# Packs of the first tokens and weights moved whole, gate columns with the biases, and a new order, in a gated mix of a spectral filter and an MLP

## The chip, the cores and the metric

The kernel runs on one core of one Trainium2 chip. The metric is the device time of one execution in microseconds (us). Before the change it is 372.66 us, the median of three runs (372.43 to 373.08).

## The reference

```python
def _A_ref(x, w_r, w_i):
    B, S, D = x.shape
    X = rfft2(x, axes=(-2, -1))
    W = w_r + 1j * w_i
    X = X * W
    return irfft2(X, (S, D), axes=(-2, -1))

def _B_ref(x, w1, b1, w2, b2):
    h = einsum("bsd,df->bsf", x, w1) + b1
    h = gelu(h)                                   # tanh form
    return einsum("bsf,fd->bsd", h, w2) + b2

x = A_x                                           # 1 x 2048 x 512
g = sigmoid((x * gate_w).sum(-1, keepdims=True))
return g * A_ref(x, A_w_r, A_w_i) + (1 - g) * B_ref(x, B_w1, B_b1, B_w2, B_b2)
```

x has 2048 tokens of 512 features, the MLP has 1792 hidden features. All arrays are float32.

## The kernel before

**Precision.** Each float32 operand of a matmul is split into a high part (names ending in h) and a low part (ending in l), both in the 12-bit format fp32r, and a product is made of three: high by high, high by low, low by high. A rounding to the high part is a copy with a cast, on ScalarE (ACT) or VectorE (DVE); the low part is a subtraction on DVE. TensorE (PE) does all products.

**The work.** The MLP is done for four columns of tokens c of 512 tokens, each made of four blocks of 128 tokens (j = c, c+4, c+8, c+12), and in two halves of seven blocks of 128 hidden features (f). For each f there is an up-product of 12 matmuls of 512 columns (tile ph, weights wa), a gelu with the bias b1t (line 1182, in place in ph), a split into g_h and g_l, and down-products (tile po, weights wb). The spectral part makes for each block j a transform along the features (tile pd, tables cf; two more columns of cf hold the gate's weights, so that the gate's logits come out of the same product), one along the tokens (py), radix-4 stages and the filter on DVE, and the way back (pz, pa). Both are mixed with the gate and written to out.

**How the order is made.** `tile_kernel` lists steps with an engine, a cost, a delay, the buffers that they read and write, and a rank (`Graph.add`). `Graph.schedule` (line 224) then plays the steps through with these costs; each engine takes the ready step of lowest rank. The ranks are the table RANKS (line 347), one number for each step, which replaces the ranks given at the steps (lines 1314 to 1316). The result is a fixed order of instructions for each engine; a number of the table tells a reader nothing by itself. SP (SyncE) issues nearly all transfers, in its own order; a transfer waits there until one of eight places for transfers under way is free and until its target buffer has been read.

**The start.** TensorE first multiplies zeros (`warm`, line 609; ZEROS = 8 products of 512 columns into the tile none). The first up-products need four packs of 256 KB:
- xa and xb hold the blocks 0 and 4 of the tokens; xa has the first two quarters q of the features, xb the last two. xa comes as two transfers of 128 KB, the first issued by ACT (line 624), the second by SP (line 625). xb (line 626) carries in each row four columns of the gate's weights besides its 512 numbers.
- war0 and war1 hold the weights of f = 0 and f = 1; war0 has the quarters 0 and 1, war1 the quarters 2 and 3 (`load_pack`, line 1101). war0 comes as two transfers of 128 KB, one for each f (line 1112), war1 as one (line 1108).

`split_packs` (line 676) rounds the packs: xa one half on ACT, one on DVE (lines 685, 686), xb on ACT (line 687). `load_pack` rounds war0 in two halves on ACT (line 1117), war1 one half on DVE and one on ACT (lines 1115, 1117). In `mlp` (line 1149) the up-products of f = 0 and 1 in column 0 are cut into passes of 12 matmuls of 256 columns: the first needs xa and war0, the second xb and war1, and two more need the tokens xr8 and xr12 (blocks 8 and 12). In the rows of the order and the profile, mxh and mxl are the split tokens, wa0h, wa0l, wa1h, wa1l the split packs of weights.

From xb's gate columns DVE works out the gate's columns of cf (gs, gq, lines 638 to 652). b1t, the biases, is loaded in `load_small` (line 655).

Of the kernel before, what the change touches and what calls it, by code (L numbers as in the profile page):

```python
# [17 lines left out]
P = 128  # L18
# [100 lines left out]
ZEROS = 8  # L119
# [56 lines left out]
class Graph:  # L176
# [281 lines left out]
)  # L458


# [907 lines left out]
```

## Time and profile before

| | |
|---|---|
| median of three runs | 372.66 us (372.43 to 373.08) |
| the profiled execution | 372.77 us, its span 370.8 us |
| instructions | 5551 |
| PE, PEld, DVE, ACT, POOL busy | 363.5, 307.4, 325.8, 235.2, 44.1 us |
| granted TensorE clock, mean | 0.998 |
| read from and written to HBM | 38.64 MB, 23.73 MB |

The span is the time from the first to the last instruction of the profiled execution; 2.0 us of its 372.77 lie around it. PE is TensorE's matmuls, PEld its weight loads, which run beside them. L12 is line 12 of the kernel; most matmuls stand under L536, a helper, so they are told apart by tile. Rows of the timeline give start, length (both us), engine, line, operation, output<-input, shape and count, and in brackets the idle time before with what ended it. In the chain of waits each row is start, length and what. Matmuls overlap, so the length of a row is longer than the distance to the next. A row of busy time by stretch gives the stretch, its length, the busy time of PE, PEld, DVE, ACT and POOL (with counts), the granted clock, the share of the DMA engines' time and GB/s.

### The profile page before, as it was taken

What the parts mean: (1) busy time and instruction counts of PE and PEld (TensorE: products, weight loads), DVE (VectorE), ACT (ScalarE), POOL (GpSimd) and SP (SyncE); (2) the same over time, 40 slices, a digit from 0 to 9 for tenths busy, and PEclk for the clock granted to TensorE, in tenths of its full rate; (3) what the DMA queues carried; (4) which work ended last, traced back from release to release, by engine and by line L of the source; (5) the groups of instructions that cost most, each with busy time, mean ns of one, the idle gap of its engine ahead of it and who ended that gap; (6) DMA issues with size and microseconds to landing.
All of it is one profiled execution on the core that took longest, in us unless ns stands there. A gap on an engine that the chain in (4) does not pass through costs nothing.

```text
span 370.8 us, 5551 instructions
## 1 busy us (share of the span) xinstructions
PE 363.5 (98%) x1799; PEld 307.4 (83%) x1799; DVE 325.8 (88%) x691; ACT 235.2 (63%) x464; POOL 44.1 (12%) x54
## 2 busy tenths in 40 slices
PE   7999999999999999999999999999999999999994
PEld 5888888888888888888888888888888888888894
DVE  4999889999999779999999999788738885999995
ACT  5875788887669755354456322796497639748830
POOL 0000000000000001111022011000432123111041
PEclk9999999999999999999999999999999999999999
DMA  7972879434934323878399684207997899825378
GB/s 236 397 244 64 253 245 361 140 100 150 311 107 138 101 60 102 216 148 194 115 204 246 175 195 67 49 14 292 180 167 130 176 300 209 138 72 115 98 99 186
DMA packets 39916, 62.99 MB, mean 170 GB/s; under 512 B 4688, under 2 KB 17552, under 8 KB 39120
## 3 DMA queue, kind: packets, MB, share of 16 engines
q1 hardware_dynamic: 32544, 49.67, 41.1%
q0 software_dynamic: 7200, 12.85, 23.7%
q8 instruction: 14, 0.23, 0.2%
q10 hardware_dynamic: 144, 0.13, 0.1%
q14 instruction: 14, 0.11, 0.1%
HBM read 38.64 MB, written 23.73 MB: 168 GB/s over the span
## 4 chain that ended last, share of the span: by engine, by line
PE 95%; DVE 1%; DMA 1%; SPq 0%; ACT 0%; issue 0%
PE ph L536 41%; PE po L536 40%; PE pz L536 4%; PE pd L536 4%; PE pa L536 3%; PE py L536 3%; DMA xb<-in_x0g 1%; DVE uv L1039 0%; DVE y L1061 0%; SPq L1112 0%; DVE o L1249 0%; DVE o L1244 0%; DVE y L1058 0%; ACT mxh L687 0%; ACT od L1036 0%
## 5 line engine op out<-in xcount | busy, mean ns | idle before, releaser
L1182 ACT ACTIVATE ph<-ph,b1t 128x512 f32<-128x512 f32 x56 | 36.9, 658 | 57.1 <-PE ph L536 54.8
L993 DVE SCALAR_TENSOR_TENSOR pq<-y,al,sw 128x256 f32<-128x256 f32 x32 | 14.0, 481 | 11.3 <-ACT sw L989 7.3
L986 ACT ACTIVATE sw<-y,al 64x512 f32<-64x512 f32 x32 | 22.5, 719 | 0.8 <-DVE y L849 0.3
L945 DVE TENSOR_TENSOR m<-y,wf 128x514 f32<-128x514 f32 x32 | 20.4, 689 | 0.0
L527 POOL DMA_DIRECT2D wa7l<-in_w x1 | 1.0, 1015 | 146.2 <-PE po L536 146.2
L527 POOL DMA_DIRECT2D bacc<-o x12 | 10.6, 931 | 65.8 <-ACT o L1231 64.6
L1228 ACT ACTIVATE o<-po,b2t 128x512 f32<-128x512 f32 x16 | 10.8, 688 | 8.3 <-PE po L536 8.3
L1231 ACT ACTIVATE o<-po 128x512 f32<-128x512 f32 x12 | 7.1, 597 | 13.6 <-PE po L536 13.3
L799 ACT ACTIVATE y<-py 64x256 f32<-64x256 f32 x32 | 12.2, 380 | 4.1 <-PE py L536 3.6
L536 PEld LDWEIGHTS pd<-cf,eoh 128*128 128x128 f32 x64 | 11.2, 188 | 2.4 <-issue 0.5
L536 PE MATMUL pd<-cf,eoh 128*128 128x260 f32 x64 | 13.1, 289 | 0.0
L796 ACT ACTIVATE y<-py 64x256 f32<-64x256 f32 x32 | 12.1, 378 | 0.5
L1039 DVE TENSOR_TENSOR uv<-pa,od 128x512 f32<-128x512 f32 x16 | 10.8, 685 | 0.5 <-ACT od L1036 0.3
L1036 ACT ACTIVATE od<-pa 128x512 f32<-128x512 f32 x8 | 4.8, 598 | 9.5 <-PE pa L536 9.3
L726 DVE TENSOR_TENSOR eo<-xr 128x256 f32<-128x256 f32 x28 | 10.8, 417 | 0.0
L536 PE MATMUL pd<-cf,eol 128*128 128x130 f32 x64 | 10.6, 251 | 0.0
L536 PEld LDWEIGHTS pd<-cf,eol 128*128 128x128 f32 x64 | 10.1, 188 | 0.2
L989 ACT ACTIVATE sw<-y 1x512 f32<-1x512 f32 x16 | 9.8, 627 | 0.4
L745 DVE TENSOR_TENSOR eol<-xr,eoh 128x512 fp32r<-128x512 f32 x12 | 8.2, 688 | 2.1 <-ACT eoh L744 2.0
L742 DVE TENSOR_TENSOR xr<-eo 128x256 f32<-128x256 f32 x24 | 9.7, 419 | 0.2
L527 POOL DMA_DIRECT2D out<-ba x8 | 7.0, 873 | 19.1 <-DVE ba L1083 7.6
L674 DVE TENSOR_TENSOR mxl<-xm,mxh 128x512 fp32r<-128x512 f32 x12 | 8.1, 686 | 1.3 <-ACT mxh L673 1.2
(717 smaller groups left out, 1339.0 us busy)
## 6 DMA issues: line engine op xcount, KB each, us to landing
wf<-in_wf SPq DMA_DIRECT2D x16, 257.0 KB, 3.6
bacc<-o SPq DMA_DIRECT2D x16, 256.0 KB, 3.1
xr<-in_xt SPq DMA_DIRECT2D x14, 256.0 KB, 3.4
wbr<-in_w SPq DMA_DIRECT2D x14, 256.0 KB, 3.7
war<-in_w SPq DMA_DIRECT2D x13, 256.0 KB, 4.5
xm<-in_xt SPq DMA_DIRECT2D x12, 256.0 KB, 5.3
bacc<-o POOLq DMA_DIRECT2D x12, 256.0 KB, 5.5
ba<-bacc SPq DMA_DIRECT2D x12, 256.0 KB, 2.7
```

What stands on the lines that cost most here:

```text
L527: return add("pool", kb / 150, 3.4, lambda: nc.gpsimd.dma_start(dst(), src(), accum_op=ALU.add), reads, writes, rank)
L536: pe.matmul(ps, w, x, start=start, stop=stop)
L726: v(lambda s=s, op=op: vec.tensor_tensor(eo.ap()[:, s], x.ap()[:, 0:2] if x else pack(0)[:, j // 4], x.ap()[:, 2:4] if x else pack(1)[:, j ...
L796: a(lambda o=o, i=i: act.activation(apart(0, o, HP), py.ap()[i:i + HP, 1].rearrange("p (a b) -> p a b", a=2), AF.Copy), HD, [py], [(Y[j], ...
L799: a(lambda o=o, i=i: act.activation(Y[j].ap()[o:o + HP, 1, :HD], py.ap()[i:i + HP, 0], AF.Copy, scale=-1.0), HD, [py], [(Y[j], 1 + k)], 0, ...
L945: v(lambda mk=mk, k=k, y=y, w=w: vec.tensor_tensor(mk.ap(), y.ap()[:, :, :ND], w.ap()[:, k:k + 1, :ND].to_broadcast([P, 2, ND]), op=ALU.mu ...
L986: a(lambda sw=sw, y=y, o=o, i=i: act.activation(sw.ap()[o:o + HP], y.ap()[i:i + HP, ::-1, :HD], AF.Copy, scale=al.ap()[i:i + HP, 0:1]), 51 ...
L989: a(lambda sw=sw, y=y, j=j: act.activation(sw.ap()[HP:HP + 1], y.ap()[HP:HP + 1, ::-1, :HD], AF.Copy, scale=math.cos(math.pi * j / NJ)), 5 ...
L993: v(lambda sw=sw, pq_=pq_, y=y, j=j, k=k, op=op: vec.scalar_tensor_tensor(pq_.ap()[:, k], y.ap()[:, k, :HD], al.ap()[:, 1 + j:2 + j], sw.a ...
L1039: v(lambda i=i, op=op: vec.tensor_tensor(uv.ap()[:, :, i], ps.ap()[:, 0], od.ap(), op=op), 512, [ps, od], [(uv, i)], 2)
L1182: a(lambda f=f, ps=ps: act.activation(ps.ap(), ps.ap(), AF.Gelu_apprx_tanh, bias=b1t.ap()[:, f:f + 1]), 600, [b1t], [ps], 0.9 if half else ...
L1228: a(lambda o=o, ps=ps, q=q: act.activation(o.ap(), ps.ap(), AF.Identity, scale=-1.0, bias=b2t.ap()[:, q:q + 1]), 600, [b2t, ps], [o])
```

## The change

xa, xb, war0 and war1 each come as one transfer of 256 KB, with the arrays laid out on the host so that each is contiguous. xa is issued whole by ACT, the other three by SP. The four gate columns move from xb into b1t, whose load is put ahead of the tables cf; gs is worked out from b1t. xa is rounded whole by DVE; war1 is rounded in two halves by ACT; the low part of war0 is one subtraction in place of two. One more product of zeros is made. RANKS is another table, so the order of all engines is another.

```diff
--- before.py
+++ after.py
@@ -116,7 +116,7 @@
 SPARE = 0.4
 LATE_SUMS = 1.5
 SOON, SPARE_SOON = 9.0, 0.05
-ZEROS = 8
+ZEROS = 9
 LATE_X = 1
 FOLD_DMA = 16
 RING, TI, TTAB = 3, 3, 3
@@ -345,116 +345,116 @@
 
 
 RANKS = (
-    -12312, -8112, -8674, 633, -8711, -11188, -8567, -11292, -9604, 821, 28, 1653, 2308, 731, 3074, 20, 536, -776,
...
+    -7460, -11155, -8172, -325, -8181, -8896, -8776, -8458, -190, 742, -779, 427, -287, 2439, 1452, 1057, 2055, 171,
...
 )
@@ -526,8 +526,8 @@
         reads = [*reads, buf("ring", [1], cls=len(g.steps))]
         return add("pool", kb / 150, 3.4, lambda: nc.gpsimd.dma_start(dst(), src(), accum_op=ALU.add), reads, writes, rank)
 
-    def dma_act(emit, kb, reads, writes):
-        return add("act", 0.4, kb / 390 + 2.2, emit, reads, writes, 0)
+    def dma_act(emit, reads, writes, lag):
+        return add("act", 0.4, lag, emit, reads, writes, 0)
 
     def raw(dst, src, q=sp):
         return q.dma_start(dst.bitcast(F32), src)
@@ -555,7 +555,7 @@
     def cf_of(c):
         return [(cft, c), (cft, 2), (cft, 3)]
 
-    b1t = one("b1t", [P, NF], pool=sa)
+    b1t = one("b1t", [P, NF + NQ], pool=sa)
     rev = one("rev", [P, NJ, 2, 2])
     b2t = one("b2t", [P, NQ])
     al = one("al", [P, 1 + NJ])
@@ -612,21 +612,21 @@
 
     add("pe", 0.427 * ZEROS + 0.05, 0.1, warm, [zero], [none], 0)
 
-    xa, xb = buf("z", [P, 2, 2, P], F32, "xa", parts=2), buf("xr", [P, D + NQ], F32, "xb")
+    xa, xb = buf("z", [P, 2, 2, P], F32, "xa", parts=2), buf("xr", [P, D], F32, "xb")
 
     def pack(k):
-        return xb.ap()[:, :D].rearrange("p (t q n) -> p t q n", t=2, q=2) if k else xa.ap()
+        return xb.ap().rearrange("p (t q n) -> p t q n", t=2, q=2) if k else xa.ap()
 
     def xblock(o, n):
         return x0g[o:o + P * n].rearrange("(p n) -> p n", n=n)
 
     add("vec", 0.2, 0.1, clear, [], Y, 0.7)
-    dma_act(lambda: act.dma_start(xa.ap()[:, 0].rearrange("p q n -> p (q n)"), xblock(0, HD)), 129, [], [(xa, 0)])
-    dma(lambda: sp.dma_start(xa.ap()[:, 1].rearrange("p q n -> p (q n)"), xblock(P * HD, HD)), 128, [], [(xa, 1)], 0, 2.5)
-    dma(lambda: sp.dma_start(xb.ap(), xblock(P * D, D + NQ)), 256, [], [xb], 0.02, 3.0)
+    dma_act(lambda: act.dma_start(xa.ap().rearrange("p t q n -> p (t q n)"), xblock(0, D)), [], [xa], 3.5)
+    dma(lambda: sp.dma_start(xb.ap(), xblock(P * D, D)), 256, [], [xb], 0.06, 3.3)
     XF = {}
     for j in NORD[2:4]:
         XF[j] = load_x(j)
+    dma(lambda: sp.dma_start(b1t.ap(), b1), 7, [], [b1t], 0.45)
     for c in range(2):
         dma(lambda c=c: raw(cft.ap()[:, c], cf_d[c]), 272, [], [(cft, c), (cft, 2), (cft, 3)], 0.6)
 
@@ -635,7 +635,7 @@
 
 
     for k, op in enumerate((ALU.add, ALU.subtract)):
-        tiny(lambda k=k, op=op: vec.tensor_tensor(gs.ap()[:, k], xb.ap()[:, D:D + 2], xb.ap()[:, D + 2:], op=op), [xb],
+        tiny(lambda k=k, op=op: vec.tensor_tensor(gs.ap()[:, k], b1t.ap()[:, NF:NF + 2], b1t.ap()[:, NF + 2:], op=op), [b1t],
              [(gs, k)])
     for k, op in enumerate((ALU.add, ALU.subtract)):
         tiny(lambda k=k, op=op: vec.tensor_tensor(gq.ap()[:, 0::3] if k else gq.ap()[:, 1:3], gs.ap()[:, :, 0], gs.ap()[:, :, 1], op=op),
@@ -652,7 +652,6 @@
     tiny(lambda: vec.tensor_tensor(gcol(1), four(), gcol(0), op=ALU.subtract), [gq, (cft, 2)], [(cft, 3)])
 
     def load_small():
-        dma(lambda: sp.dma_start(b1t.ap(), b1), 7, [], [b1t], 0.45)
         dma(lambda: sp.dma_start(b2t.ap(), b2), 2, [Y[0]], [b2t])
         add("vec", 0.1, 0.1, lambda: vec.tensor_scalar(b2t.ap(), b2t.ap(), -1.0, None, op0=ALU.mult), [], [b2t], 3)
         dma(lambda: sp.dma_start(rev.ap(), wrev), 32, [Y[0]], [rev])
@@ -682,8 +681,7 @@
         def both(b, k):
             return [(b, k), (b, 2 + k)]
 
-        a(lambda: act.activation(part(h, 0, 0), xa.ap()[:, 0], AF.Copy), 256, [(xa, 0)], [(h, 0)], 0)
-        v(lambda: vec.tensor_copy(part(h, 0, 1), xa.ap()[:, 1]), 256, [(xa, 1)], [(h, 2)], 0)
+        v(lambda: vec.tensor_copy(part(h, 0), pack(0)), 340, [xa], both(h, 0), 0)
         a(lambda: act.activation(part(h, 1), pack(1), AF.Copy), 512, [xb], both(h, 1), 0)
         for k, b in enumerate((xa, xb)):
             v(lambda k=k: vec.tensor_tensor(part(l, k), pack(k), part(h, k), op=ALU.subtract), 512, [b, *both(h, k)], both(l, k), 0)
@@ -1104,22 +1102,11 @@
             t = buf("wra", [P, D], F32, f"war{k}", parts=2)
             h, l = (buf("wa", [P, D], F32R, f"wa{k}{i}", parts=2) for i in "hl")
             PACK.append((h, l))
-            if k:
-                dma(lambda t=t: sp.dma_start(t.ap(), w1[1]), 256, [], [t], 0.05, 3.2)
+            dma(lambda k=k, t=t: sp.dma_start(t.ap(), w1[k]), 256, [], [t], 0.05 + k / 10, 3.2 if k else 3.0)
             for f in range(2):
                 u = slice(f * HD, (f + 1) * HD)
-                if not k:
-                    dma(lambda f=f, u=u, t=t: sp.dma_start(t.ap()[:, u], w1[0].rearrange("p d -> (p d)").rearrange("(f p d) -> f p d", f=2, d=HD)[f]),
-                        128, [], [(t, f)], 0.05, 2.8 + 0.2 * f)
-                if k and not f:
-                    v(lambda u=u, t=t, h=h: vec.tensor_copy(h.ap()[:, u], t.ap()[:, u]), HD, [(t, f)], [(h, f)], EARLY - 0.1)
-                else:
-                    a(lambda u=u, t=t, h=h: act.activation(h.ap()[:, u], t.ap()[:, u], AF.Copy), HD, [(t, f)], [(h, f)], EARLY - 0.1)
-                if not k:
-                    v(lambda u=u, t=t, h=h, l=l: vec.tensor_tensor(l.ap()[:, u], t.ap()[:, u], h.ap()[:, u], op=ALU.subtract), HD,
-                      [(t, f), (h, f)], [(l, f)], EARLY - 0.1)
-            if k:
-                v(lambda t=t, h=h, l=l: vec.tensor_tensor(l.ap(), t.ap(), h.ap(), op=ALU.subtract), D, [t, h], [l], EARLY - 0.1)
+                a(lambda u=u, t=t, h=h: act.activation(h.ap()[:, u], t.ap()[:, u], AF.Copy), HD, [(t, f)], [(h, f)], EARLY - 0.1)
+            v(lambda t=t, h=h, l=l: vec.tensor_tensor(l.ap(), t.ap(), h.ap(), op=ALU.subtract), D, [t, h], [l], EARLY - 0.1)
         for f in range(2):
             W["a", f] = None
 
@@ -1336,11 +1323,10 @@
     w1 = np.asarray(B_w1)[fold].reshape(NQ, P, NF, P).transpose(2, 1, 0, 3).reshape(NF, P, D)
     w2 = np.asarray(B_w2)[:, DORD].reshape(NF, P, D)
     b2 = np.asarray(B_b2)[DORD].reshape(NQ, P).T
-    b1 = np.asarray(B_b1).reshape(NF, P).T
     gw = np.asarray(gate_w)[fold].reshape(NQ, P).T
-    x0g = [xt[j, :, 2 * k:2 * k + 2].reshape(P, HD) for k in range(2) for j in (0, NJ // 4)]
-    x0g = np.concatenate([x0g[0].ravel(), x0g[1].ravel(), np.concatenate([*x0g[2:], gw], 1).ravel()])
-    w1 = np.concatenate([w1[:2, :, :HD].reshape(1, P, D), w1[:2, :, HD:].transpose(1, 0, 2).reshape(1, P, D), w1[2:]])
+    b1 = np.concatenate([np.asarray(B_b1).reshape(NF, P).T, gw], 1)
+    x0g = np.stack([xt[:NJ // 2:NJ // 4, :, 2 * k:2 * k + 2].transpose(1, 0, 2, 3) for k in range(2)]).ravel()
+    w1 = np.concatenate([np.stack([w1[:2, :, k * HD:(k + 1) * HD].transpose(1, 0, 2).reshape(P, D) for k in range(2)]), w1[2:]])
     wf = np.stack([np.asarray(A_w_r), np.asarray(A_w_i)], 1)
     back = (-np.arange(S)) % S
     rows = (P * np.arange(NJ)[:, None] + KROW) % S
```

SP's transfers at the start, before (war_93 and war_96 are war0 and war1, xr_100 and xr_105 the tokens xr8 and xr12, war_109 and wbr_113 the weights of f = 2 and of the first down-product):

```order
L625 DMA xa<-in_x0g 128x256
L1112 DMA war_93<-in_w 128x256 x2
L1108 DMA war_96<-in_w 128x512
L626 DMA xb<-in_x0g 128x516
L594 DMA xr_100<-in_xt 128x512
L594 DMA xr_105<-in_xt 128x512
L1140 DMA war_109<-in_w 128x512
L1140 DMA wbr_113<-in_w 128x512
L655 DMA b1t<-in_b 128x14
L1140 DMA wbr_131<-in_w 128x512
```

SP's transfers at the start now (war_78 and war_97 are war0 and war1, xr_99 and xr_101 xr8 and xr12):

```order
L1105 DMA war_78<-in_w 128x512
L625 DMA xb<-in_x0g 128x512
L1105 DMA war_97<-in_w 128x512
L594 DMA xr_99<-in_xt 128x512
L594 DMA xr_101<-in_xt 128x512
L1127 DMA war_103<-in_w 128x512
L1127 DMA wbr_105<-in_w 128x512
L629 DMA b1t<-in_b 128x18
L1127 DMA wbr_114<-in_w 128x512
L533 DMA cf<-cf 128x544
```

Five issues before xr8 became three, and xb went from the last of them to the second; war1 is now the last.

ACT at the same place, before (mxh_102 is the high part of the tokens):

```order
L624 DMA xa<-in_x0g 128x256
L606 ACT_TABLE_LOAD
L606 ACTIVATE gate<-zero 128x1
L685 ACTIVATE mxh_102<-xa 128x256
L1117 ACTIVATE wa0h<-war_93 128x256 x2
L1117 ACTIVATE wa1h<-war_96 128x256
L687 ACTIVATE mxh_102<-xb 128x2x256
L673 ACTIVATE mxh_102<-xr_100 128x512
```

ACT now:

```order
L624 DMA xa<-in_x0g 128x512
L606 ACT_TABLE_LOAD
L606 ACTIVATE gate<-zero 128x1
L1108 ACTIVATE wa0h<-war_78 128x256 x2
L685 ACTIVATE mxh_111<-xb 128x2x256
L1108 ACTIVATE wa1h<-war_97 128x256 x2
L672 ACTIVATE mxh_111<-xr_99 128x512
```

The rounding of xa left ACT, that of xb stands ahead of war1's, and both halves of war1 are ACT's.

TensorE's first passes, before (ph_0 and ph_1 are the up-products of f = 0 and f = 1):

```order
L536 MATMUL none<-zero 128x512 x8
L536 MATMUL ph_0_117<-mxh_102,wa0h 128x256 x2
L536 MATMUL ph_0_117<-mxl_107,wa0h 128x256 x2
L536 MATMUL ph_0_117<-mxh_102,wa0l 128x256 x2
L536 MATMUL ph_1_128<-mxh_102,wa0h 128x256 x2
L536 MATMUL ph_1_128<-mxl_107,wa0h 128x256 x2
L536 MATMUL ph_1_128<-mxh_102,wa0l 128x256 x2
L536 MATMUL ph_1_128<-mxh_102,wa1h 128x256 x2
L536 MATMUL ph_0_117<-mxh_102,wa1h 128x256 x2
L536 MATMUL ph_0_117<-mxl_107,wa1h 128x256 x2
L536 MATMUL ph_0_117<-mxh_102,wa1l 128x256 x2
```

TensorE's first passes now:

```order
L536 MATMUL none<-zero 128x512 x9
L536 MATMUL ph_0_118<-mxh_111,wa0h 128x256 x2
L536 MATMUL ph_1_124<-mxh_111,wa0h 128x256 x2
L536 MATMUL ph_0_118<-mxl_116,wa0h 128x256 x2
L536 MATMUL ph_1_124<-mxl_116,wa0h 128x256 x2
L536 MATMUL ph_0_118<-mxh_111,wa0l 128x256 x2
L536 MATMUL ph_1_124<-mxh_111,wa0l 128x256 x2
L536 MATMUL ph_1_124<-mxh_111,wa1h 128x256 x2
L536 MATMUL ph_1_124<-mxl_116,wa1h 128x256 x2
L536 MATMUL ph_0_118<-mxh_111,wa1h 128x256 x2
L536 MATMUL ph_0_118<-mxl_116,wa1h 128x256 x2
L536 MATMUL ph_1_124<-mxh_111,wa1l 128x256 x2
```

In the first pass f = 0 and f = 1 now alternate, where all of f = 0 stood first. In the second pass ph_1 with mxh and wa1h still opens; mxl follows after two products where it followed after four, and all eight products with wa1h now stand ahead of those with wa1l.

218 rows, old and new, of the table RANKS are left out of this document.

## The prediction

> **What bounds the kernel now.** I read the page's shares and its strip of slices first, then the list of what TensorE waited for, then the chain that ended last, then the first ten microseconds by engine.
>
> ```profile
> span 370.8 us, 5551 instructions
> PE 363.5 (98%) x1799; PEld 307.4 (83%) x1799; DVE 325.8 (88%) x691; ACT 235.2 (63%) x464; POOL 44.1 (12%) x54
> PE   7999999999999999999999999999999999999994
> PE 95%; DVE 1%; DMA 1%; SPq 0%; ACT 0%; issue 0%
> ```
>
> TensorE (PE) is busy in every slice but the first and the last. What it waited for, in the whole run, is three things, all at the start:
>
> ```profile
> PE ph L536 <- ACT mxh L687: 1.1, 1, 1.1
> PE none L536 <- DVE zero L604: 1.1, 1, 1.1
> PE ph L536 <- ACT wa0h L1117: 0.4, 1, 0.4
> ```
>
> The chain over the first 9 us (start, length, what) and over the end:
>
> ```profile
> 2.60 4.69 DMA xb<-in_x0g
> 7.31 0.64 ACT mxh L687
> 8.00 0.74 PE ph L536 x4
> ...
> 361.11 0.61 ACT od L1036
> 361.74 1.30 DVE uv L1039 x2
> ...
> 366.68 0.42 DVE o L1249
> ```
>
> So the time has three parts: the transfer of xb and its rounding on ScalarE up to 8.00; 353 us of matmuls without a wait; and a tail of some 10 us after 361.11. Both orders hold the same matmuls, but for one more warm-up product. A change at the start therefore moves the end by as much as it moves the point from which TensorE runs without a pause, if the new order keeps it fed.
>
> **Where that point is now.** TensorE's own rows (start, length, operation, idle before):
>
> ```profile
> 1.06 3.59 PE L536 MATMUL none<-zero 128*128 128x512 f32 x8 [1.06 <-DVE zero L604]
> 4.49 0.40 PE L536 MATMUL ph<-mxh,wa0h 128*128 128x256 f32 x2
> 8.00 0.74 PE L536 MATMUL ph<-mxh,wa1h 128*128 128x256 f32 x4 [1.14 <-ACT mxh L687]
> 9.32 0.40 PE L536 MATMUL ph<-mxl,wa1h 128*128 128x256 f32 x2
> 9.56 0.40 PE L536 MATMUL ph<-mxh,wa1l 128*128 128x256 f32 x2
> 9.80 0.40 PE L536 MATMUL ph<-mxh,wa0h 128*128 128x256 f32 x2
> ```
>
> A pair of 256-column products takes 0.24 (9.32 to 9.56 to 9.80), so 0.12 each. The products come in passes: first 12 that need the packs xa and war0, then 12 that need xb and war1 too, and at 9.80 the third pass, with the tokens xr8 and xr12. Twelve unhindered products take 1.44, so the second pass ran as if it had begun at 9.80 - 1.44 = 8.36.
>
> **What arrives when.** Busy time per stretch; the last column is GB/s of all transfers:
>
> ```profile
> 1.80:3.30 1.50, 1.50 (x5) 1.17 (x4) 0.01 (x1) 0.86 (x2) 0.00 (x0) 1.00 0.82 276
> 3.30:5.40 2.10, 2.10 (x10) 1.63 (x8) 1.31 (x3) 0.72 (x2) 0.00 (x0) 1.00 0.84 156
> 5.40:7.30 1.90, 1.06 (x7) 0.76 (x6) 0.72 (x2) 0.83 (x2) 0.00 (x0) 1.00 0.99 363
> 50.00:100.00 50.00, 50.00 (x252) 42.33 (x251) 48.12 (x115) 40.55 (x105) 0.00 (x0) 1.00 0.65 213
> ```
>
> The rate reaches 276, falls to 156 for 2.1 us, and is 363 afterwards. By 7.3, when xb is there, 1.5 x 276 + 2.1 x 156 + 1.9 x 363 = 1430 kB have come, of which xa, war0, war1 and xb are 1050; the other 380 belong to transfers issued behind them. Had the hole run at 363, the same bytes would have been there 1.2 us sooner.
>
> **The change, part by part.**
>
> The issues on SP (SyncE's queue):
>
> ```profile
> 0.74 0.39 SPq L625 DMA_DIRECT2D xa<-in_x0g  x1
> 1.19 0.89 SPq L1112 DMA_DIRECT2D war<-in_w  x2
> 2.12 0.43 SPq L1108 DMA_DIRECT2D war<-in_w  x1
> 2.60 0.46 SPq L626 DMA_DIRECT2D xb<-in_x0g  x1
> ```
>
> An issue takes about 0.45 whether it moves 128 KB or 256. Now two of five are gone: war0 goes out at 0.74, xb at 1.19, war1 at 1.65, all done at 2.08 instead of 3.06. The bytes of the four packs stay the same (the gate columns, 2 KB, leave xb). What was last is xb; now it is war1, issued 0.95 earlier than xb was (2.60 to 1.65).
>
> When war1 lands is the one large unknown. Lower bound: no hole and nothing from behind mixed in, 414 kB by 3.30 and the other 640 at 363, so 5.05. Upper bound: as late as xb now, 7.29, the sum of bytes being the same. Issues lay 0.45 apart while only 128 KB went with each, so part of the hole may be a lack of issued work, and part transfers that stood. I take the hole half filled, at (156 + 363)/2 = 260: it moves 546, so 960 kB are there by 5.40. Needed are the 1050 and between half and all of the 380 that mix in, 1240 to 1430 kB; at 363 that is 6.2 to 6.7, of which I take 6.5.
>
> What follows the landing on ScalarE and VectorE:
>
> ```profile
> 5.42 0.42 ACT L1117 ACTIVATE wa0h<-war 128x256 fp32r<-128x256 f32 x1 [1.24 <-DMA war<-in_w]
> 7.94 1.33 ACT L673 ACTIVATE mxh<-xr 128x512 fp32r<-128x512 f32 x2
> 3.29 0.29 DVE L686 CAST mxh<-xa 128x256 fp32r<-128x256 f32 x1 [2.19 <-DMA xa<-in_x0g]
> 3.90 0.70 DVE L689 TENSOR_TENSOR mxl<-xa,mxh 128x512 fp32r<-128x512 f32 x1 [0.32 <-ACT mxh L685]
> ```
>
> ScalarE now rounds both halves of war1, 2 x 0.42 = 0.84, where VectorE used to take one half; the second pass begins with the second half (ph_1 with wa1h). It starts at 6.5 + 0.84 + 0.05 = 7.39, the 0.05 being the step from ScalarE's end at 7.95 to TensorE's 8.00. That is 8.36 - 7.39 = 0.97 earlier. ScalarE rounds xb ahead of that, 0.64; xb is a whole pack ahead of war1, 262 kB at 363 or 0.72, so this is out of the way with 0.08 to spare, and what is lacking there adds to the start. mxl of xb takes VectorE up to 0.70 from about 6.45 and is needed at 7.39 + 0.24, so the small halt after the first four products (8.00 to 8.74), which was for it, should go; wa1l takes VectorE up to 0.70 after wa1h and is needed 8 x 0.12 = 0.96 after. I keep 0.07 of the gain back for such edges: -0.9.
>
> What hides the rest. The first pass starts later: xa and war0 now land whole and share the engines, 524 kB at 414 by 3.30 and 260 after that, so about 3.7, against 3.29 for the halves. The cast of the whole xa on VectorE is bounded by 0.29 and 0.70; nearer to the cast, I take 0.45. Then mxl ends at 4.85 and wa0l at 5.55. The warm-up, 4.65 now, ends at 4.9 to 5.1 (one product more, between the 0.24 of two 256-column ones and 3.59/8 = 0.45), so the pass runs from 5.0 to 6.44. The second pass waits for war1 until 7.39 in any case: cover 0.95. Without it, each 0.1 of delay costs 0.1. The third pass is due at 7.39 + 1.44 = 8.83; ScalarE has xr8 and xr12 rounded 1.33 after 7.34, at 8.67: cover 0.16, and xr12 has to be there by 8.0. Two more transfers at 363, 0.72 each, land at 7.2 and 7.9. That is thin; it can cost 0 to 0.3, which the range holds.
>
> The gate columns now come with b1t, whose issue waits on SP until xa has landed; behind it stand wbr1, cf and the xm loads. VectorE takes gs only behind wb0l. Bounds: nothing, or a halt of VectorE of some tenths that stays within its slack. I take 0.
>
> The tail. After the last matmul pass VectorE has the same operations as now, with one y moved behind the first pair of o; none is added and the last is the same 0.42 one: 0, give or take 0.1.
>
> Sum: the profiled execution, 372.77, minus 0.9 is 371.9. The median of the three runs is 372.66, so 371.9 is 0.2% under it; 0.2%, 0.75 us, is about what a measurement of this kernel can tell from no change.
>
> **The rivals.**
>
> *No hole (0.20).* The hole was only lack of issued work. Then war1 lands at 5.05, wa1h is ready at 5.95, and the first pass's end at 6.44 is the bound: 8.36 - 6.44 = 1.92, so 370.8. For it: fewer, larger transfers, issued a microsecond earlier. Against it: xb, issued at 2.60, took 4.69 though the rate was low meanwhile; something stood. The Trainium skill (SBUF — State Buffer, The DMA setup-cost knee) gives a transfer about 2 us fixed plus its bytes at 436 GB/s, by which a 256 KB pack is 2.6 us and one large transfer beats two; it would put war1 at about 4.3 and the result at this rival's 370.8, an estimate from that page. The trace does not agree with it at the start: 4.69 for xb.
>
> *The landing stays (0.19).* The hole has its length whatever is issued. war1 lands at 7.29, the second pass starts at 8.19, gain 0.17: 372.6, no change.
>
> *Slower: war1 late (0.09).* More bytes are issued when the hole begins, so more stand in it, and war1, the third on its queue and beside the whole xa on ScalarE's queue, lands later than xb did. Break-even is a landing at 7.47; from 8.2 on it is slower by over 0.2%. With another microsecond in the hole, 8.3, the second pass starts at 9.2: 373.6. The Trainium skill (DMA: Bandwidth & Descriptors, Issuing engines are not separate DMA queues) says that transfers of all issuing engines run on the same 16 engines and interleave; that speaks for this rival. No row here shows two whole packs on two queues.
>
> *Slower: the new order (0.10).* VectorE is busy 48.12 of the 50 us from 50 to 100, with 1.88 idle, and TensorE does not wait once. An order that puts three more subtracts of 0.6 ahead of one that TensorE needs takes that away: a wait of 1.8, less the 0.9 gained, gives 373.7. Against it: in these 50 us the order of now got by without one wait, with VectorE just as full.
>
> **How the numbers follow.** The forecast has 0.42, and its own range is 371.2 to 372.5 (landing 5.9 to 7.1). About 0.25 of it lies beyond 0.2% and 0.17 within. Faster: 0.25 + 0.20 = 0.45. Same: 0.17 + 0.19 = 0.36. Slower: 0.19. The range takes in the rival without a hole and both slower prices: 370.6 to 373.6.
>
> **What would show it.** In the new profile: xb issued at about 1.2 and war1 at 1.65; the rate between 3.3 and 5.4 well over 156; the wait ahead of the second pass released by wa1h, not by mxh of xb; the third pass at about 8.8 instead of 9.80; no other wait of TensorE; and the chain's tail from od as long as now. I am wrong if war1 lands at 7.3 or later, if TensorE waits anywhere after 10 us, or if the first pass, not the second, sets the start.

## The result, and the profile after

The changed kernel takes 371.14 us, the median of 13 runs (370.51 to 371.67). The kernel before, run beside it, takes 372.92 (13 runs, 372.10 to 374.63). The ratio is 0.995, 95% interval 0.9938 to 0.9962: faster by 0.5%, or 1.8 us. The forecast was 371.9, within 370.6 to 373.6. The direction held; the forecast gain, 0.75 us, was less than half of what came. Two single executions of the experiments below, 2085.57 us and 404.39 us, lie far above all others of their kernels and are left out of the ranges and ratios there, not out of the medians.

The profiled execution after took 371.67, the longest of its 13, against 372.77 before. The shares of the page are those of before, one warm-up product more:

```profile
span 369.8 us, 5553 instructions
PE 364.0 (98%) x1800; PEld 307.8 (83%) x1800; DVE 325.7 (88%) x689; ACT 232.9 (63%) x464; POOL 44.2 (12%) x54
```

What TensorE waited for besides the zeros of its warm-up (total, times, longest):

```profile
PE ph L536 <- ACT wa0h L1108: 0.4, 1, 0.4
PE py L536 <- DVE x0l L775: 0.2, 1, 0.2
```

The wait of 1.1 for xb's rounding is gone. The wait for wa0h, ahead of the first pass, is left, and there is a new one for x0l at 32 us. The chain over the first 12 us and at the end (start, length, what):

```profile
0.74 4.05 DMA war<-in_w
4.79 0.02 issue
4.82 0.73 ACT wa0h L1108 x2
5.55 0.06 issue
5.60 5.83 PE ph L536 x44
...
360.63 0.61 ACT od L1034
...
366.24 0.42 DVE o L1236
```

It begins with war0, which was hidden before, and runs from 5.60 on through 44 products without a break. Before, it began with xb and reached TensorE at 8.00. From od to the end of the last subtract it is 366.66 - 360.63 = 6.03, and was 367.10 - 361.11 = 5.99: VectorE's end is as long as it was. The rows of the first 9 us (start, length, operation, idle before it):

```profile
0.73 0.41 ACTq L624 DMA_DIRECT2D xa<-in_x0g  x1
0.74 0.40 SPq L1105 DMA_DIRECT2D war<-in_w  x1
1.20 0.41 SPq L625 DMA_DIRECT2D xb<-in_x0g  x1
1.65 0.43 SPq L1105 DMA_DIRECT2D war<-in_w  x1
5.03 0.43 DVE L684 CAST mxh<-xa 128x512 fp32r<-128x512 f32 x1 [3.93 <-DMA xa<-in_x0g]
5.49 0.69 DVE L687 TENSOR_TENSOR mxl<-xa,mxh 128x512 fp32r<-128x512 f32 x1
5.57 0.63 ACT L685 ACTIVATE mxh<-xb 128x512 fp32r<-128x512 f32 x1
6.10 0.68 DVE L1109 TENSOR_TENSOR wa0l<-war,wa0h 128x512 fp32r<-128x512 f32 x1
6.23 0.72 ACT L1108 ACTIVATE wa1h<-war 128x256 fp32r<-128x256 f32 x2
6.84 0.74 PE L536 MATMUL ph<-mxh,wa0l 128*128 128x256 f32 x4
7.42 0.40 PE L536 MATMUL ph<-mxh,wa1h 128*128 128x256 f32 x2
8.86 0.28 PE L536 MATMUL ph<-mxh,wa0h 128*128 128x256 f32 x1
```

The issues are where the diff puts them. xa was there only at 5.03. ScalarE went from xb (ended 6.20) to war1 (6.23) with no idle time, so war1 was there by then. The second pass began at 7.42, the third at 8.86 instead of 9.80. The rate per stretch (last column, GB/s):

```profile
1.80:3.30 1.50, 1.50 (x5) 1.17 (x4) 0.00 (x0) 0.86 (x2) 0.00 (x0) 1.00 0.86 172
3.30:5.40 2.10, 1.95 (x5) 0.99 (x3) 0.37 (x1) 0.58 (x2) 0.00 (x0) 1.00 1.01 371
```

The hole between 3.30 and 5.40 (156 before) is not half filled but gone. Instead the first stretch fell from 276 to 172, so a low rate has moved to an earlier place. From 1.80 to 5.40 it is 1.50 x 172 + 2.10 x 371 = 1037 kB in all, where the kernel before had 742 and the prediction took 960.

Two more differences lie behind the start. The last product of TensorE before, and then a wait on the way and the last product after:

```profile
365.83 0.28 PE L536 MATMUL po<-g_13h,wb13l 128*128 128x256 f32 x1
```

```profile
32.00 0.50 PE L536 MATMUL py<-x0l,tf 128*128 128x512 f32 x1 [0.24 <-DVE x0l L775]
...
365.36 0.28 PE L536 MATMUL po<-g_13h,wb13l 128*128 128x256 f32 x1
```

From the third pass to the last product it is 365.83 - 9.80 = 356.03 before and 365.36 - 8.86 = 356.50 after: 0.47 of the 0.94 was lost on the way, in this execution, part of it in the wait at 32.00. And from the end of the last subtract to the end of the span it is 370.8 - 367.10 = 3.70 before and 369.8 - 366.66 = 3.14 after: 0.56 came at the end, where the prediction had put 0.

### The profile page after: what moved, and what is told of

Its sections match the earlier page's. It is cut to its first block, busy times and chain, and to the rows that moved or that the text cites. A ratio compares the mean times of both kernels' runs of the same rounds, so it can differ in the third digit from the quotient of the medians.

```text
span 369.8 us, 5553 instructions
## 1 busy us (share of the span) xinstructions
PE 364.0 (98%) x1800; PEld 307.8 (83%) x1800; DVE 325.7 (88%) x689; ACT 232.9 (63%) x464; POOL 44.2 (12%) x54
## 4 chain that ended last, share of the span: by engine, by line
PE 90%; DVE 4%; DMA 3%; issue 1%; ACT 1%; DVEq 0%
PE po L536 39%; PE ph L536 38%; PE pz L536 4%; PE pd L536 3%; PE pa L536 3%; PE py L536 3%; DMA wbr<-in_w 1%; DMA war<-in_w 1%; DVE uv L1037 0%; DVE y L1059 0%; DVE eo L724 0%; DVE cl L740 0%; DVE o L1236 0%; DVE y L1056 0%; DVE eol L743 0%
## 5 line engine op out<-in xcount | busy, mean ns | idle before, releaser
L536 PE MATMUL pd<-cf,eoh 128*128 128x260 f32 x64 | 12.3, 286 | 0.0
L527 POOL DMA_DIRECT2D out<-ba x8 | 7.9, 1060 | 14.2 <-DVE ba L1081 7.8
```

Source lines behind the costliest of these rows:

```text
L527: return add("pool", kb / 150, 3.4, lambda: nc.gpsimd.dma_start(dst(), src(), accum_op=ALU.add), reads, writes, rank)
L536: pe.matmul(ps, w, x, start=start, stop=stop)
```

## The experiments

Three theories stood at the outset. S: the gain comes from the transfers at the start, whole packs instead of halves. O: it comes from the new order and the place of the gate columns. T: it comes from the end, where the last six steps of VectorE and SP (two y, two pairs of o) stand in another order. The ratios below are against the kernel before, run in the same sitting (medians 372.91 to 373.26), with 95% intervals; gains in us that follow a ratio are worked out from it. The edits are shortened, and some are put in words; the dots stand for what is left out.

**Whole packs alone** (before_whole): the kernel before, its order and its gate columns, with xa and war0 each in one transfer.

```diff
-    dma_act(lambda: act.dma_start(xa.ap()[:, 0]..., xblock(0, HD)), 129, [], [(xa, 0)])
-    dma(lambda: sp.dma_start(xa.ap()[:, 1]..., xblock(P * HD, HD)), 128, [], [(xa, 1)], 0, 2.5)
+    dma_act(lambda: act.dma_start(xa.ap()..., xblock(0, D)), 129, [], [(xa, 0)])
+    dma(lambda: None, 128, [], [(xa, 1)], 0, 2.5)
...
-   sp.dma_start(t.ap()[:, u], w1[0]...[f])
+   None if f else sp.dma_start(t.ap(), w1[0])
```

> The kernel before with its own order, table and gate columns; only xa and war0 come whole (xa by ACT, war0 by SP; the two places of the second halves issue nothing). Theory S, the start: the gain of the changed kernel comes from the packs' transfers, so most of it is here too: the second pass no longer waits for the rounding of xb, the third pass starts at 8.7 to 9.2 instead of 9.80, and the time is 0.7 to 1.2 us under before. Rival O, the order: the gain comes from the new order (its tail, its spacing); then this is within 0.3 us of before.

Measured: 371.70 (371.39 to 372.02), ratio 0.996 (0.9948 to 0.9972), 1.5 us faster. Its rate in the stretch of the hole, and then its third pass and last product on TensorE:

```profile
3.30:5.40 2.10, 1.81 (x7) 0.98 (x5) 1.06 (x3) 1.21 (x4) 0.00 (x0) 1.00 0.95 289
```

```profile
8.72 0.40 PE L536 MATMUL ph<-mxh,wa0h 128*128 128x256 f32 x2
...
364.80 0.28 PE L536 MATMUL po<-g_13h,wb13l 128*128 128x256 f32 x1
```

The third pass is 1.08 earlier than before; from there to the last product it is 356.08, as before. Theory S carries most of the gain by itself, more than the 0.7 to 1.2 us expected, though the interval overlaps that of the whole change. The rate is 289 where there were 156. But this rate alone does not set the start: two later runs, before_newtail and before_no_last_add, issue the same transfers at the start as the kernel before, and their rows of this stretch are

```profile
3.30:5.40 2.10, 2.10 (x8) 1.71 (x7) 1.32 (x3) 1.10 (x3) 0.00 (x0) 1.00 0.82 258
3.30:5.40 2.10, 2.10 (x8) 1.71 (x7) 1.39 (x4) 1.14 (x3) 0.00 (x0) 1.00 0.86 271
```

In before_no_last_add the higher rate brought nothing: the second pass starts at 7.97 and the third at 9.77, against 8.00 and 9.80 before. In before_newtail the second is earlier, at 7.48, but the third waits for xr12 until 10.26. What the edit of before_whole is sure to change is the time of issue. xb, the last pack, goes out at 1.65 instead of 2.60, and its rounding starts at 5.89 instead of 7.31. Whether the larger transfers also run better was not separated from this.

**The new order with halves** (after_halves): the changed kernel with xa and war0 in halves of 128 KB again.

```diff
-    dma_act(lambda: act.dma_start(xa.ap()..., xblock(0, D)), [], [xa], 3.5)
+    def two_xa():
+        act.dma_start(xa.ap()[:, 0]..., xblock(0, HD))
+        sp.dma_start(xa.ap()[:, 1]..., xblock(P * HD, HD))
+    dma_act(two_xa, [], [xa], 3.5)
...
+   for f in range(2): sp.dma_start(t.ap()[:, f * HD:(f + 1) * HD], w1[0]...[f])
```

> The changed kernel with its order, only xa and war0 come in halves of 128 KB again (xa one half by ACT, one by SP; war0 two by SP). Theory S: the issues of xb and war1 go out 0.9 us later and the hole in the rate may be back; the second pass waits for wa1h, the third pass starts at 9.5 or later instead of 8.86, and the time is 0.7 to 1.2 us over the changed kernel, 372.0 where before is 372.9. Rival O: it stays within 0.3 us of the changed kernel, 1.5 to 1.9 under before.

Measured: 372.00 (371.28 to 373.03), ratio 0.9971 (0.996 to 0.9982), 1.1 us faster than before. War1, issued at 2.59 instead of 1.65, is the transfer in its chain now:

```profile
2.59 4.36 DMA war<-in_w
...
6.97 0.73 ACT wa1h L1119 x2
```

```profile
3.30:5.40 2.10, 1.97 (x5) 0.99 (x3) 1.12 (x2) 0.63 (x2) 0.00 (x0) 1.00 0.80 215
```

```profile
9.28 0.40 PE L536 MATMUL ph<-mxh,wa0h 128*128 128x256 f32 x2
...
365.03 0.28 PE L536 MATMUL po<-g_13h,wb13l 128*128 128x256 f32 x1
```

Behind the chain stand the rate in the stretch of the hole, and TensorE's third pass and last product. With the halves the rate there is 215, and the third pass is later than in the changed kernel. But 1.1 us stay, which S does not explain: the third pass is still 0.52 earlier than before, the way to the last product is 355.75 (0.28 less), and the end is shorter (3.06 after the last subtract, not 3.70). The two parts do not add up: 1.5 and 1.1 alone, 1.8 together. Theory O has a share, clear with halves; what the order adds to whole packs, 1.8 less 1.5, lies within the intervals. The profiled execution of after_halves is its shortest (371.28) and that of the changed kernel its longest (371.67), so a difference between these two profiles is not the difference of the kernels.

**The end** (after_oldtail, before_newtail): the last six steps moved, in the changed kernel to where they stood before, in the kernel before to where they stand now.

```diff
+    move(("y", 0), ("y", 1))            # after_oldtail
+    move(("yout", 1), ("y", 0))
+    move(("yout", 0), ("yout", 1))
...
+    move(("o", 3, 0), ("y", 0))         # before_newtail
+    move(("t", 3, 0), ("o", 3, 0))
+    move(("y", 1), ("t", 3, 0))
```

> The changed kernel, only its last steps in the order of before: both y sums and both y stores ahead of the four o operations and the two o stores. Theory T, a part of the gain is the tail (the chain's last operation to the end of the span was 3.70 us before and 3.14 after): this is 0.4 to 0.6 us over the changed kernel. Rival: the tail's 0.56 is chance of one execution; this is within 0.2 us of the changed kernel, 1.6 to 2.0 under before. The start is that of the changed kernel: its profile also shows whether first packets stand for about 0.9 us each time.

> The kernel before, only its last steps in the order of the changed kernel: a y sum, o, o, a y sum, o, o, and the stores y, o, y, o. Theory T: 0.4 to 0.6 us under before. Rival: within 0.2 us of before. The start is that of before: its profile also shows whether the hole in the rate between 3.3 and 5.4 us (156 GB/s) comes again.

Measured: 371.17 (370.52 to 371.56), ratio 0.9943 (0.9931 to 0.9956), and 373.34 (372.39 to 375.09), ratio 1.0004 (0.9991 to 1.0017). Neither differs from its parent: the order of the last six steps is worth nothing that can be told, and T falls in that form.

**Which pack** (after_xa_halves, after_war0_halves): the changed kernel with one of the two edits of after_halves.

> The changed kernel with xa alone in two transfers of 128 KB (the second on SP ahead of war0); war0 whole, order kept. Both packs in halves gave 372.0 and both whole 371.1. Theory of the issues (each transfer more on SP puts all behind it 0.45 us back): half of that loss, 371.5 us, war0 issued at 1.19, xb at 1.65, war1 at 2.1, third pass at about 9.1 us. Rival, xa's halves are the whole of it (the rounding waits for the later of two queues): 372.0 us. Rival, war0 alone decides: 371.1 us, third pass at 8.86.

> The changed kernel with war0 alone in two transfers of 128 KB, xa whole on ScalarE's queue, order kept. Theory of the issues: 371.5 us, as with xa alone in halves, since xb and war1 go out 0.45 us later there too. Rival, war0's halves are the whole of it: 372.0 us, third pass at 9.3. Rival, xa alone decides: 371.1 us.

Measured: 372.23 (371.24 to 372.52), ratio 0.9971 (0.9959 to 0.9982), and 371.62 (370.77 to 373.04), ratio 0.9966 (0.9955 to 0.9978). The intervals overlap, so the two aren't told apart. By the ratios each alone costs 0.6 to 0.8 us against the changed kernel and both together 0.8, where the theory of the issues gave each half. This is not firm: the intervals also reach into that of the changed kernel (0.9938 to 0.9962), and the profiles show no later start. Their third passes begin at 8.71 and 8.46, before the 8.86 of the changed kernel, and not at the 9.1 expected for xa. These profiles are of short executions (371.24 and 370.85); where the others lose the time is not shown. A half in either place gives 0.9966 to 0.9971; with whole packs the new order gives 0.9943 to 0.9961 in six kernels.

**The gate columns, and the order of issue** (after_gates_xb, after_war1_first, before_xb_first):

```diff
-    xb = buf("xr", [P, D], F32, "xb")                      # after_gates_xb
+    xb = buf("xr", [P, D + NQ], F32, "xb")
-    gs ... b1t.ap()[:, NF:NF + 2], b1t.ap()[:, NF + 2:]
+    gs ... xb.ap()[:, D:D + 2], xb.ap()[:, D + 2:]
...
-    sp: xb, war1                                           # after_war1_first
+    sp: war1, xb
...
-    sp: war1, xb                                           # before_xb_first
+    sp: xb, war1
```

> The changed kernel with the gate columns behind xb again (rows of 2064 instead of 2048 bytes); packs whole, every engine's order kept. The changed kernel with both packs in halves still stood 1.1 us below the kernel before. Theory that the gate columns carry this: 372 us or more, xb landing later and the second pass waiting for mxl or the rounding of xb. Rival, the columns are worth nothing, as the prediction has it: 371.1 us within 0.4.

> The changed kernel with war1 issued ahead of xb on SP, as before; packs whole, everything else kept. Theory that xb ahead of war1 is worth part of the gain (xb feeds the second pass by its rounding and mxl): xb lands about 0.5 us later, ScalarE rounds war1 behind it, the second pass starts at about 7.9 instead of 7.42, 371.6 us. Rival, the start is set by the first pass and the 0.45 us of either fit under it: 371.1 us.

> The kernel before with xb issued ahead of war1 on SP (the two trade places), packs in halves and everything else as before. With its packs in halves the changed kernel still stood 1.1 us below the kernel before; its own start had xb ahead of war1. Theory that the place of xb carries most of this when the packs are in halves: 372.3 us against 373.0, third pass near 9.3 us instead of 9.8, and war1 half a microsecond later. Rival, the place of xb is worth nothing here either (it was worth nothing with whole packs): 373.0 us, and the 1.1 us lie behind the start, in the new order.

Measured: 371.13 (four runs, 371.03 to 371.36), ratio 0.9947 (0.9934 to 0.996); 371.18 (370.57 to 371.88), ratio 0.995 (0.9935 to 0.9964); and 373.89 (373.02 to 375.05), ratio 1.0022 (1.0009 to 1.0035). The gate columns are worth nothing that can be told, and so is the order of xb and war1 in the changed kernel. In the kernel before, xb first is slower by 0.8 us, where both theories had it faster or the same. Its rows show a part of that:

```profile
7.20 0.42 ACT L1120 ACTIVATE wa1h<-war 128x256 fp32r<-128x256 f32 x1 [1.80 <-DMA war<-in_w]
7.52 0.61 ACT L689 ACTIVATE mxh<-xb 128x512 fp32r<-128x512 f32 x1
8.19 0.74 PE L536 MATMUL ph<-mxh,wa1h 128*128 128x256 f32 x4 [1.76 <-ACT mxh L689]
```

The order on ScalarE still had war1 first. ScalarE stood 1.80 for a war1 that now came later, with xb's rounding queued behind, and the third pass starts at 10.05, 0.25 later than before. Order of issue and order of use should agree; the change turned both. The rest is not at the start: in this profile the end of the span comes 4.43 after the last subtract instead of 3.70, in the same order of steps.

**The warm-up, and xb on ScalarE's queue** (after_8_zeros, after_xb_act):

```diff
-        for _ in range(ZEROS):                             # after_8_zeros
+        for _ in range(ZEROS - 1):
...
-    dma_act(lambda: act.dma_start(xa...), [], [xa], 3.5)   # after_xb_act
-    dma(lambda: sp.dma_start(xb...), 256, [], [xb], 0.06, 3.3)
+    dma_act(two, [], [xa], 3.5)       # two: act issues xa, then xb
+    dma(lambda: None, 256, [], [xb], 0.06, 3.3)
```

> The changed kernel with eight products on zeros instead of nine, everything else in place. The ninth only fills TensorE's wait (nine end at about 5.2 us, the first pass starts between 5.0 and 5.6): no change, 371.1 us, the first pass where the transfers put it. Rival, the ninth delays a first pass that is ready by 5.0 in the better executions: 370.9 us. Rival, the idle gap lowers the granted clock: 371.5 us or more.

> The changed kernel with xb issued by ScalarE behind xa, so that SP issues war0 and war1 first and all its later loads 0.45 us earlier; the table load on ScalarE moves 0.45 us back, still ahead of the first rounding. A try at a faster version. If the issues of SP limit the start: war1 out at 1.20, xb at 1.18, third pass 0.2 to 0.4 us earlier, 370.8 us. Rival, the rate of the first 1 MB limits it, which the order of issue does not change: 371.1 us.

Measured: 371.32 (370.33 to 372.66), ratio 0.9961 (0.9944 to 0.9977), and 371.03 (370.42 to 373.09), ratio 0.9951 (0.9934 to 0.9969). Neither can be told from the changed kernel. With xb on the other queue war1 is issued by 1.60 and everything behind it earlier, the first pass still waits for war0, and the third starts at 8.96, no earlier than 8.86:

```profile
4.72 0.72 ACT L1112 ACTIVATE wa0h<-war 128x256 fp32r<-128x256 f32 x2 [1.57 <-DMA war<-in_w]
5.50 0.74 PE L536 MATMUL ph<-mxh,wa0h 128*128 128x256 f32 x4 [0.61 <-ACT wa0h L1112]
```

So it is no longer the issues that set the start. The Trainium skill (DMA: Bandwidth & Descriptors, Issuing engines are not separate DMA queues) says that transfers from all issuing engines run on the same 16 engines; by that another queue buys nothing once the work is out, and this run agrees (371.03 against 371.14).

**The adds at the end** (before_no_last_add). In the traces the end of the span follows the last subtract by 3.5 to 4.4 us in four profiles of the old order and by 2.7 to 3.5 in nine of the new. The last run leaves out the last accumulating store of GpSimd's queue, in the kernel before:

```diff
-            acc(lambda: part(c, h, 1), lambda: flat(n), 256, [n], [(OUT[c], 2 * h + 1)], 4)
+            s = acc(lambda: part(c, h, 1), lambda: flat(n), 256, [n], [(OUT[c], 2 * h + 1)], 4)
+            if (c, h) == (1, 0):
+                s.emit = lambda: None
```

> The kernel before without its last accumulating store (the 256 KB of -uv that GpSimd's queue adds to the output 3.4 us ahead of the last product); that summand is left out of one quarter of one output, everything else and the order is kept. In four profiles of the old order 156 to 178 KB of these adds were still moving after the last product and the end came 3.5 to 4.4 us after the last subtract; in nine of the new order 28 to 124 KB and 2.7 to 3.5. Theory that the adds still moving push the last plain stores back: the end comes 3.0 us or less after the last subtract, and the time falls by 0.5 to 1.0, to about 372.2. Rival, the last stores' own latency sets the tail: 3.5 to 4.4 us as before, and 373.0.

Measured: 372.15 (eleven runs, 371.77 to 373.35), ratio 0.997 (0.9956 to 0.9985): 1.1 us faster. The start is that of before (third pass at 9.77), and so is the way to the last product (356.01). Its last subtract and its span:

```profile
366.63 0.42 DVE o L1251
```

```profile
span 370.1 us, 5549 instructions
```

The end comes 370.1 - 367.05 = 3.05 after the last subtract instead of 3.70; both figures miss the expected ones narrowly (3.0 or less, a gain of 0.5 to 1.0) and are far from the rival's. Transfers in the microseconds after the last product (the last two columns are the busy share of the DMA engines and GB/s): before, before without the add, and after.

```profile
365.80:366.80 1.00, 0.31 (x3) 0.11 (x1) 0.97 (x4) 0.00 (x0) 0.00 (x0) 1.00 0.88 166
366.80:367.80 1.00, 0.00 (x0) 0.00 (x0) 0.30 (x1) 0.00 (x0) 0.00 (x0) 1.00 1.00 348
367.80:368.80 1.00, 0.00 (x0) 0.00 (x0) 0.00 (x0) 0.00 (x0) 0.00 (x0) 1.00 1.03 377
368.80:369.80 1.00, 0.00 (x0) 0.00 (x0) 0.00 (x0) 0.00 (x0) 0.00 (x0) 0.86 0.22 76
```

```profile
365.80:366.80 1.00, 0.26 (x3) 0.05 (x1) 0.97 (x4) 0.00 (x0) 0.00 (x0) 1.00 0.61 227
...
367.80:368.80 1.00, 0.00 (x0) 0.00 (x0) 0.00 (x0) 0.00 (x0) 0.00 (x0) 1.00 0.54 186
```

```profile
365.40:366.40 1.00, 0.23 (x2) 0.03 (x1) 0.97 (x3) 0.00 (x0) 0.00 (x0) 1.00 0.96 271
...
367.40:368.40 1.00, 0.00 (x0) 0.00 (x0) 0.00 (x0) 0.00 (x0) 0.00 (x0) 1.00 0.63 228
```

Before, the engines are busy 88% of the first microsecond and move 166 GB/s; the plain stores reach into the fourth. Without the add, and in the changed kernel, the engines are down to 54% and 63% in the third. The first microsecond by queue (packets, MB, share of the 16 engines' time; q0 is GpSimd's, with the adds, q1 is SP's, with the plain stores), before and then without the add:

```profile
q0 software_dynamic: 79, 0.15, 85.1%
q1 hardware_dynamic: 6, 0.01, 3.3%
```

```profile
q1 hardware_dynamic: 111, 0.23, 60.6%
```

The adds held the DMA engines while the plain stores hardly began. For the same share of the engines the adds moved about half as much: 0.15 MB for 85.1%, against 0.23 MB for 60.6%. So T holds in another form: not the last six steps, but the adds still moving behind the last product set the length of the end. That one add fewer shortens the end is shown. That it has to be an add is not: no plain store of the same size was left out instead. By these rows, as an estimate, it would have held the engines for about half the time. Which part of the new order lets the adds finish earlier was not tried. An earlier issue of the last one it is not: the last add goes out at 362.38 before, 3.45 ahead of the last product, and at 362.15 after, 3.21 ahead.

## Why the prediction came out as it did

*The issues.* Right: war0 at 0.74, xb at 1.20, war1 at 1.65, all out by 2.08.

*The hole, "half filled" at 260.* Wrong. It measured 371, as in the rival without a hole, while the stretch ahead of it fell from 276 to 172. Whether the hole of before was a lack of issued work or transfers that stood stays open. Against a lack of work alone speaks the prediction's own row, which it read for its rate only: the engines' share was 0.84 at 156 GB/s, and the four packs of 1050 kB were all issued by 3.06, when 414 kB had come by 3.30. And a higher rate alone did not make the start earlier: with the same transfers it was 271 in before_no_last_add, and the third pass was at 9.77.

*War1 at 6.5, its rounding 0.84.* Early enough not to count: it was there by 6.23 and its rounding took 0.72.

*xa and war0 at 3.7, the first pass at 5.0, "cover 0.95".* This step failed. They landed at 5.03 and 4.79, the first pass began at 5.60, and it was paced by VectorE behind xa: cast 0.43, mxl 0.69, wa0l 0.68, up to 6.78, and four products then lead to 7.42. So the pass took 1.82, where 1.44 was put. The step took 414 kB by 3.30, the 276 GB/s of before; there were 172 GB/s, 258 kB. The first pass set the start, one of the three signs named for being wrong.

*The start, 7.39 and 8.83.* Measured 7.42 and 8.86, so the term of 0.9 is right to 0.05, but by luck: two errors cancel, war1 earlier than thought and the first pass later. The mechanism at the start is that of the rival without a hole, with its first pass 0.6 late and 0.38 longer. In the other profiles with whole packs the third pass is at 8.63 to 9.21. In one of them, after_gates_xb, the second pass does wait for wa1h as forecast (0.29, until 7.68).

*The matmuls between, 0.* In the profiled execution 0.47 was lost, with a wait of 0.24 for x0l at 32.00, the second sign named. Most of it is not the order's: in six of the nine profiles of the new order the same stretch took 355.74 to 355.77, in the others 355.97, 356.18 and the 356.50 here, against 356.01 to 356.15 in the five of the old. So where it runs undisturbed the new order is about 0.28 shorter here, which the prediction had put at 0; what in the order does it is not known. The rival of VectorE starving TensorE after 50 us did not come.

*The tail, "0, give or take 0.1".* This term was mis-sized, and it is the largest part of what the forecast lacked: 0.56 in the profile. The step counted VectorE's operations, which are indeed the same, and not the transfers that the end waits for. before_no_last_add shows that one of the adds at the end is worth 1.1 us.

With the start at 0.94, the matmuls at 0.28 and the end at 0.56 the sum is 1.78, the difference of the medians; the profiled execution, with its 0.47 lost instead, comes to 0.94 - 0.47 + 0.56 = 1.03 of its 1.10. The first sum draws the 0.28 from other kernels' traces, and the end alone varies by more than its term (3.5 to 4.4 in the old order, 2.7 to 3.5 in the new). So it is an account and not a proof, and that it meets the medians so closely is luck.

*The range.* It was said to take in both slower prices, but ends at 373.6 where one of them is 373.7. Nothing came of this.

*The covers that held.* The gate columns 0 (371.13 with them back), the ninth warm-up product hidden (371.32 without it, within the noise), xr8 and xr12 in time for the third pass, and the order of the last six steps 0.

The Trainium skill (SBUF — State Buffer, The DMA setup-cost knee) has one large transfer beat two, by a fixed 2 us of each. In direction the runs agree: 1.5 us with whole packs in the old order, 0.6 to 0.8 us lost by the ratios with a half in either pack. In size they do not at the start, where war0's 256 KB took 4.05 us against 2.6, an estimate from the page's figure.

## What to carry to other kernels

When a start waits on several small transfers, look at when the last one it needs is issued: two issues fewer put it out 0.95 us earlier, and whole packs brought 1.5 us. A low rate in one profile is not yet a cause; compare profiles with the same transfers first (156, 258 and 271 here; at 271 the third pass was 0.03 earlier than at 156). Turn the order of issue and the order of use together, or the engine that uses them stands behind the wrong one (0.25 us at the start here). At the end, count the transfers still moving behind the last product, above all accumulating ones, before calling the tail unchanged.

## What had not been expected of the hardware

In the first microsecond of transfers the changed kernel moved almost nothing. In its first half the engines were occupied (a share of 1.10; the times of packets are added up, so it can exceed 1), in its second half mostly idle (0.22), though xa and war0 had been issued at 0.73 and 0.74. The same kernel with gate columns behind xb again (after_gates_xb, below it) did not show that:

```profile
1.80:2.30 0.50, 0.50 (x3) 0.40 (x2) 0.00 (x0) 0.50 (x1) 0.00 (x0) 1.00 1.10 53
2.30:2.80 0.50, 0.50 (x2) 0.40 (x2) 0.00 (x0) 0.36 (x2) 0.00 (x0) 1.00 0.22 82
```

```profile
1.80:2.30 0.50, 0.50 (x3) 0.40 (x2) 0.00 (x0) 0.50 (x1) 0.00 (x0) 1.00 0.47 123
2.30:2.80 0.50, 0.50 (x2) 0.40 (x2) 0.00 (x0) 0.36 (x2) 0.00 (x0) 1.00 1.02 393
```

Between 2.30 and 2.80 the rate was 82 to 172 GB/s in all six profiles with xa whole and xb without the gate columns, and 270 to 393 in the eight others. Whether row length, the place of the arrays in memory or chance makes it stays open; the times of the two kernels above are the same (371.14 and 371.13), so it bought nothing to be without it.
